# Moving the late weights' low parts from GpSimd to VectorE, and re-queuing the transfers around them

## The chip, the core and the metric

The kernel runs on one core of one Trainium2 chip. The metric is the device time of one launch in microseconds (us). The engines are TensorE (PE in the profile; PEld is its weight load), VectorE (DVE), ScalarE (ACT), GpSimd (POOL) and SyncE (SP), which issues DMAs only. ScalarE and GpSimd can issue DMAs too.

## The reference

Three stages follow one another on 2304 tokens of 512 columns, all in float32:

```
x = decay_attention(q, k, v, f)                  # 4 batches, 8 heads, 576 positions, 64 columns
h = x @ w_in                                     # 512 -> 2048
y = mish(h) @ moe_w_out                          # 2048 -> 512;  mish(h) = h * tanh(softplus(h))
z = max(y @ w1, y @ w2, y @ w3) @ moe2_w_out     # 512 -> 768 -> 512
```

The weights arrive as 8-byte floats.

## The kernel before

**Products.** TensorE multiplies pairs of float32r tiles. Every operand is split into a high part (a rounded copy) and a low part (the value less the high part), and `mm3` (L183 to L187) adds three products per block: high by high, high by low, low by high.

**Weights.** `load_f32` (L148) fetches a chunk of raw words, two int32 each (tile `wr`, three buffers), and five VectorE operations (L161, L162, L165, L168, L172) make float32 of it (tile `wt`, two buffers). `split` (L136) then makes the high part on ScalarE (L138) and the low part on GpSimd (L144).

**Stages.** Attention and the product with `w_in` run interleaved until about 412 us. The rest of `h` follows; each block is copied out as `he` by ScalarE (L544) and stored to `h_d` in DRAM. Meanwhile 16 chunks of `moe_w_out` (128x512) are loaded and split through `in_turn` (L584): a chunk is converted, and the split of the chunk before it is issued behind the last `he` copy (`issue_after`).

The y stage then makes 72 steps (the loop after L670). A step loads a tile `g` of `h_d` (L656, L658, SyncE's queue, six buffers), applies Mish in place (L659, ScalarE), makes `gh` (L665, ScalarE) and `gl` (L666, VectorE), and multiplies them with a chunk of `wo` in 12 matmuls. Loads run five steps ahead and splits two. From step 9 on, every second step converts one chunk of the second block's weights (24 of 128x384 into `wa`, 6 of 128x512 into `wo2`). The converted `wa` chunks are also stored to `a_d` by ScalarE's queue. When a block of 512 tokens is done, four tiles `ze` (three buffers) are copied out of PSUM: for the first block by ScalarE (L697), for the others by ScalarE and VectorE in turn (L703, L700), with the stores to `z_d` on those tiles' own queues, ScalarE's and SyncE's.

The last stage multiplies the first 512 tokens directly (tiles g of L185 to L187 with `yh`, `yl`), and the rest by a scheme of seven products that needs sums of weight blocks. `sums_of_weights` (L752) reads `a_d` back (tile `r`, L759, SyncE's queue), adds on VectorE (L760), splits each sum in two halves on ScalarE and GpSimd (tile `sk`, two buffers), and stores it to `s_d` (L767, SyncE's queue). There are three matrices, with four loads and four stores each. The products of the scheme read `s` from `s_d` (L847, SyncE's queue); they are the matmuls q<-t,s and q<-b,s. `operands` (L717) prepares the tokens' side.

**Order.** Instructions of an engine, and DMAs of a queue, start in one fixed order. A planner draws it up: it runs through the program with a cost for each operation and takes the ready work of the highest priority. Work under `tc.high_priority(AHEAD)` goes first, and `tc.issue_after(ins)` places the work in its block behind `ins` on the same engine without a wait for its end. At run time the order stands, and whatever waits at the head of a queue holds up everything behind it.

Of the kernel before, what the change touches and what calls it, by code (L numbers as in the profile page):

```python
# [67 lines left out]
def tile_decay_attention__mish_ff__max3_ff(  # L68
# [16 lines left out]
    nc = tc.nc  # L85
# [60 lines left out]
    pace, on_act = [], []  # L146

    def load_f32(pool, srcs, bufs=None, abs_eng="dve", raw="wr"):  # L148

        m, n = len(srcs), srcs[0].shape[1]  # L150
        t = pool.tile([128, m, n], F32, name="wt", tag="wt", bufs=bufs)
        r = pool.tile([128, m, n, 2], I32, name=raw, tag=raw, bufs=3 if pool is not wst else bufs)

        with tc.issue_after(pace[-1].ins) if pace else ExitStack():
            for i, src in enumerate(srcs):
                nc.sync.dma_start(r[:, i].rearrange("p n w -> p (n w)"), src.bitcast(I32))
        lo, hi, ti = r[:, :, :, 0], r[:, :, :, 1], t.bitcast(I32)
        if abs_eng == "act":
            nc.scalar.activation(t, hi.bitcast(F32), AF.Abs)
        else:  # L160
            nc.vector.tensor_scalar(ti, hi, 0x7FFFFFFF, None, op0=ALU.bitwise_and)  # L161
        nc.vector.tensor_scalar(  # L162
            t, t, F32_MIN_AS_HIGH_HALF, F32_MAX_AS_HIGH_HALF, op0=ALU.max, op1=ALU.min
        )
        nc.vector.tensor_scalar(  # L165
            ti, ti, 3, 0x3FFFFFF8, op0=ALU.logical_shift_left, op1=ALU.bitwise_and
        )
        nc.vector.scalar_tensor_tensor(  # L168
            out=ti, in0=hi, scalar=-0x40000000, in1=ti,
            op0=ALU.bitwise_and, op1=ALU.bitwise_or,  # L170
        )
        nc.vector.scalar_tensor_tensor(  # L172
            out=ti, in0=lo, scalar=29, in1=ti,
            op0=ALU.logical_shift_right, op1=ALU.bitwise_or,
        )
        return t

    def load_split(pool, dst_hi, dst_lo, srcs, eng_hi, eng_lo, bufs=None, abs_eng="dve", raw="wr"):
        t = load_f32(pool, srcs, bufs, abs_eng, raw)
        split(dst_hi, dst_lo, t, eng_hi, eng_lo)  # L180
        return t
# [16 lines left out]
    def load_w_in():  # L198
        for fp in range(NFP):
            fs = slice(fp * 256, fp * 256 + 256)  # L200
            for c in range(0, KD, 2):
                blocks = [moe_w_in[d * 128:(d + 1) * 128, fs] for d in (c, c + 1)]
                load_split(
                    wst, wi[fp][:, 0, c:c + 2], wi[fp][:, 1, c:c + 2], blocks, "act", "pool", abs_eng="act"
                )
                yield
            loaded.add(fp)
# [303 lines left out]
    def h_steps():  # L511
# [9 lines left out]
        for n, (i, fp) in enumerate(order):  # L521
# [18 lines left out]
            if n % 2 and done < NT:  # L540
                nc.vector.tensor_copy(he, h)
                queue = nc.sync
            else:
                on_act[:] = [nc.scalar.activation(he, h, AF.Copy)]  # L544
                queue = nc.scalar
# [38 lines left out]
    def in_turn(jobs):  # L584

        last = None
        for src, hi, lo, keep in jobs:
            t = load_f32(stg2, [src])
            if last:
                finish_split(*last)  # L590
            last = (t, hi, lo, keep)
            yield
        finish_split(*last)

    def finish_split(t, hi, lo, keep):
        with tc.issue_after(on_act[-1].ins) if on_act else ExitStack():
            split(hi, lo, t, "act", "pool")
            if keep is not None:
                nc.scalar.dma_start(keep, t[:, 0])

    def load_w_out():
        return in_turn(
# [3 lines left out]
        )  # L606
# [27 lines left out]
    def load_w2():  # L634
# [14 lines left out]
        return in_turn(jobs)  # L649

    def load_g(ib, fp, a):
# [3 lines left out]
        if n == BLK2:  # L655
            nc.sync.dma_start(g, h_d[ib][fp][:, a, :])  # L656
        else:
            nc.sync.dma_start(g.rearrange("p (a n) -> p a n", a=2), h_d[ib][fp][:])  # L658
# [3 lines left out]
    def split_g(g, n, tiles):  # L662
# [3 lines left out]
        latest[:] = [nc.vector.tensor_tensor(out=gl, in0=g, in1=gh, op=ALU.subtract)]  # L666
        return [(t, (gh[:, i * n:(i + 1) * n], gl[:, i * n:(i + 1) * n])) for i, t in enumerate(tiles)]

    latest = []
# [5 lines left out]
    for step, (ib, fp, a) in enumerate(todo):  # L675
# [14 lines left out]
        if step >= 8 and step % 2:  # L690
            with tc.issue_after(latest[-1].ins):
                next(wgen3, None)
        if final:
            for j in range(KD):
                ze = zst.tile([128, n], F32, name="ze", tag="ze")
                if ib == 0:
                    nc.scalar.activation(ze, y[j], AF.Copy)  # L697
                    split(y0[0][:, j], y0[1][:, j], ze, "act", "pool")
                elif j % 2:
                    nc.vector.tensor_copy(ze, y[j])  # L700
                    nc.sync.dma_start(z_d[ib][:, j, :], ze)
                else:
                    nc.scalar.activation(ze, y[j], AF.Copy)  # L703
                    nc.scalar.dma_start(z_d[ib][:, j, :], ze)
    for _ in wgen3:
        pass

# [44 lines left out]
    def sums_of_weights(pool):  # L752

        for m in range(3):
            r = {}
            for i in range(2):
                for j in range(2):
                    r[i, j] = pool.tile([128, 2, 384], F32, name=f"r{i}{j}")
                    nc.sync.dma_start(r[i, j], a_d[m][i, j][:])  # L759
            two = lambda o, x, y, op: nc.vector.tensor_tensor(out=o, in0=x, in1=y, op=op)  # L760

            def keep(k, src):
                t = pool.tile([128, 3, 2, 2, 128], F32R, name="sk", bufs=2)
                for c in range(2):
                    with tc.issue_after(on_act[-1].ins):
                        split(t[:, :, c, 0], t[:, :, c, 1], src[:, c].rearrange("p (a f) -> p a f", a=3), "act", "pool")
                nc.sync.dma_start(s_d[m][k][:], t.bitcast(F32))  # L767
# [39 lines left out]
    for ft in range(NF2):  # L807
# [7 lines left out]
        with tc.high_priority(AHEAD):  # L815
# [5 lines left out]
            nc.vector.tensor_tensor(out=hl[ft], in0=mx, in1=hh[ft], op=ALU.subtract)  # L821
# [113 lines left out]
```

## Time and profile before

| | us |
|---|---|
| median of 3 runs (991.92 to 993.0) | 992.31 |
| profiled execution, its own time | 999.44 |
| its span | 997.7 |

| engine | busy us | share of the span |
|---|---|---|
| PE | 927.6 | 93% |
| PEld | 829.1 | 83% |
| DVE | 612.3 | 61% |
| ACT | 472.2 | 47% |
| POOL | 380.7 | 38% |

The mean granted TensorE clock was 0.974 of full speed. The profiled execution has 1.7 us around its span and is 7.1 us longer than the median of the runs without a profile. Shares are means over stages with different limits.

### The profile page before, as it was taken

What the parts mean: (1) busy time and instruction counts of PE and PEld (TensorE: products, weight loads), DVE (VectorE), ACT (ScalarE), POOL (GpSimd) and SP (SyncE); (2) the same over time, 40 slices, a digit from 0 to 9 for tenths busy, and PEclk for the clock granted to TensorE, in tenths of its full rate; (3) what the DMA queues carried; (4) which work ended last, traced back from release to release, by engine and by line L of the source; (5) the groups of instructions that cost most, each with busy time, mean ns of one, the idle gap of its engine ahead of it and who ended that gap; (6) DMA issues with size and microseconds to landing.
All of it is one profiled execution on the core that took longest, in us unless ns stands there. A gap on an engine that the chain in (4) does not pass through costs nothing.

```text
span 997.7 us, 16274 instructions
## 1 busy us (share of the span) xinstructions
PE 927.6 (93%) x5648; PEld 829.1 (83%) x5648; DVE 612.3 (61%) x1299; ACT 472.2 (47%) x1043; POOL 380.7 (38%) x427
## 2 busy tenths in 40 slices
PE   4886789999998999999999989899998999999998
PEld 4674689999998999999878777677886899889986
DVE  4868897755556647339947757577585244814440
ACT  4876666766667666433345444335343222512211
POOL 6766876656446733223304211122135332103310
PEclk8998789999999999999989999999999999999999
DMA  5455646445444531566644656665359744424411
GB/s 154 138 154 149 174 136 195 147 141 156 127 121 138 151 94 43 203 228 201 216 137 158 205 187 185 207 205 169 101 189 334 260 122 119 121 91 121 118 41 74
DMA packets 120130, 154.84 MB, mean 155 GB/s; under 512 B 35888, under 2 KB 79408, under 8 KB 120048
## 3 DMA queue, kind: packets, MB, share of 16 engines
q1 hardware_dynamic: 101360, 130.47, 42.9%
q10 hardware_dynamic: 18688, 23.34, 6.6%
q8 instruction: 44, 0.72, 0.3%
q14 instruction: 38, 0.31, 0.1%
HBM read 107.55 MB, written 46.21 MB: 154 GB/s over the span
## 4 chain that ended last, share of the span: by engine, by line
PE 52%; DVE 17%; DMA 16%; ACT 6%; issue 5%; POOL 2%; SPq 2%; ACTq 0%; DVEq 0%; POOLq 0%
DMA g<-h_d 9%; PE q L185 5%; PE q L186 5%; PE q L187 5%; PE av L453 5%; PE h L186 4%; PE h L185 4%; PE h L187 4%; PE sc L365 3%; PE pp L440 3%; DVE wt L165 3%; DVE wt L168 2%; PE tr L320 2%; PE o L185 2%; PE o L186 2%
## 5 line engine op out<-in xcount | busy, mean ns | idle before, releaser
L185 PE MATMUL h<-xh,wi 128*128 128x256 f32 x576 | 167.1, 291 | 4.3 <-ACT he L544 2.9
L186 PE MATMUL h<-xl,wi 128*128 128x256 f32 x576 | 166.9, 290 | 1.7 <-POOL xl L144 1.7
L187 PE MATMUL h<-xh,wi 128*128 128x256 f32 x576 | 165.8, 288 | 0.0
L186 PE MATMUL y<-gl,wo 128*128 128x512 f32 (+1 forms) x320 | 119.8, 374 | 3.0 <-DVE gl L666 3.0
L187 PE MATMUL y<-gh,wo 128*128 128x512 f32 (+1 forms) x320 | 118.1, 372 | 0.0
L185 PE MATMUL y<-gh,wo 128*128 128x512 f32 (+1 forms) x320 | 107.6, 376 | 9.4 <-ACT gh L665 8.0
L185 PEld LDWEIGHTS h<-xh,wi 128*128 128x128 f32 x576 | 111.3, 194 | 6.0 <-ACT he L544 3.5
L186 PEld LDWEIGHTS h<-xl,wi 128*128 128x128 f32 x576 | 111.4, 193 | 2.8 <-POOL xl L144 2.1
L187 PEld LDWEIGHTS h<-xh,wi 128*128 128x128 f32 x576 | 111.5, 194 | 0.3
L659 ACT ACTIVATE g<-g 128x512 f32<-128x512 f32 x72 | 45.2, 629 | 107.8 <-DMA g<-h_d 102.2
L666 DVE TENSOR_TENSOR gl<-g,gh 128x512 fp32r<-128x512 f32 x72 | 52.8, 734 | 62.0 <-ACT gh L665 61.3
L416 ACT ACTIVATE P<-P,mn 128x128 f32<-128x128 f32 (+3 forms) x128 | 71.0, 556 | 27.2 <-DVE mn L410 26.3
L185 PEld LDWEIGHTS y<-gh,wo 128*128 128x128 f32 x320 | 60.2, 190 | 24.3 <-ACT gh L665 12.7
L144 POOL TENSOR_TENSOR wa<-wt,wa 128x384 fp32r<-128x384 f32 x24 | 26.5, 1103 | 135.3 <-ACT wa L138 135.3
L440 PE MATMUL pp<-ident,P 128*128 128x128 f32 x320 | 61.8, 294 | 14.0 <-POOL P L390 12.8
L186 PEld LDWEIGHTS y<-gl,wo 128*128 128x128 f32 x320 | 61.1, 191 | 15.6 <-DVE gl L666 5.5
L390 POOL TENSOR_SCALAR P<-P,rr 128x128 f32<-128x128 f32 (+3 forms) x128 | 69.1, 555 | 7.0 <-DVE rr L388 3.6
L187 PEld LDWEIGHTS y<-gh,wo 128*128 128x128 f32 x320 | 61.0, 191 | 10.2
L453 PE MATMUL av<-TB,vs 128*128 128x320 f32 (+2 forms) x320 | 61.7, 311 | 4.7 <-ACT TB L447 4.2
L861 DVE TENSOR_TENSOR u<-q,p 128x448 f32<-128x448 f32 x36 | 22.4, 621 | 66.5 <-PE q L187 66.5
L320 PE MATMUL tr<-identr,qk 128*128 128x128 f32 x432 | 49.3, 257 | 13.8 <-POOL qk L144 13.8
L448 DVE TENSOR_TENSOR TB<-pp,TB 128x512 fp32r<-128x512 f32 (+1 forms) x80 | 49.0, 657 | 16.4 <-ACT TB L447 16.0
(147 smaller groups left out, 2357.7 us busy)
## 6 DMA issues: line engine op xcount, KB each, us to landing
g<-h_d SPq DMA_DIRECT2D x72, 256.0 KB, 3.5
s<-s_d SPq DMA_DIRECT2D x72, 256.0 KB, 2.9
h_d<-he ACTq DMA_DIRECT2D x46, 256.0 KB, 3.3
wr<-in_moe_w_out_dram SPq DMA_DIRECT2D x22, 512.0 KB, 4.3
wr<-in_moe_w_dram SPq DMA_DIRECT2D x24, 384.0 KB, 3.4
s_d<-sk SPq DMA_DIRECT2D x12, 768.0 KB, 4.8
cb<-cum_d SPq DMA_DIRECT2D x64, 128.0 KB, 3.4
wr<-in_moe_w_in_dram SPq DMA_DIRECT2D x32, 256.0 KB, 3.6
```

Source lines behind the costliest of these rows:

```text
L165: nc.vector.tensor_scalar(ti, ti, 3, 0x3FFFFFF8, op0=ALU.logical_shift_left, op1=ALU.bitwise_and)
L185: nc.tensor.matmul(ps, wh, xh, start=start, stop=False, skip_group_check=True)
L186: nc.tensor.matmul(ps, wh, xl, start=False, stop=False, skip_group_check=True)
L187: return nc.tensor.matmul(ps, wl, xh, start=False, stop=stop, skip_group_check=True)
L320: nc.tensor.transpose(dst[:, c:c + 128].bitcast(F32R), src, identr)
L390: nc.gpsimd.tensor_scalar(made[ci], made[ci], rr[:, ci:ci + 1], 1.0, op0=ALU.mult, op1=ALU.mult)
L416: nc.scalar.activation(Pt, Pt, AF.Exp, scale=-1.0, bias=mn[:, col - 1:col], accum_out=sm[:, ci:ci + 1],)
L440: nc.tensor.transpose(pp[:, n * 128:n * 128 + 128], Pt[:, k0:k0 + 128], ident)
L448: nc.vector.tensor_tensor(out=T[:, 1, cols], in0=src, in1=T[:, 0, cols], op=ALU.subtract)
L453: nc.tensor.matmul(avp[h][:, off:off + w], vl, T[:, i, c:c + w], start=kt == 0 and i == 0 and not (g == 0 and h == 1), stop=last and i == ...
L659: nc.scalar.activation(g, g, AF.Mish)
L666: latest[:] = [nc.vector.tensor_tensor(out=gl, in0=g, in1=gh, op=ALU.subtract)]
```

## The change

- `load_f32` becomes two functions: `fetch` issues the raw loads, `convert` does the five operations.
- For `moe_w_out` and the second block's weights the low part is made by VectorE, behind the conversion of the next chunk.
- Raw words are fetched two chunks ahead for `moe_w_out` and one ahead for the second block, there behind the last issued load of `g` (`pace`).
- The conversion and the low part are queued behind the last `gl` (or `hl`) on VectorE (`on_dve`), the high part behind the last `gh` (or `hh`) on ScalarE (`on_act`). While `moe_w_out` is loaded both lists are empty.
- All `ze` copies, and for the later blocks the `z_d` stores, go to ScalarE and its queue.
- The sums' loads and stores go to POOL's queue, which issued no DMA before. A sum is split in one operation each by ScalarE and VectorE.

```diff
-    def load_f32(pool, srcs, bufs=None, abs_eng="dve", raw="wr"):
+    pace, on_act, on_dve = [], [], []
+    def fetch(pool, srcs, bufs=None):
...
+        with queued(pace):
             for i, src in enumerate(srcs):
                 nc.sync.dma_start(r[:, i].rearrange("p n w -> p (n w)"), src.bitcast(I32))
+        return r
+    def convert(pool, r, bufs=None, abs_eng="dve"):
...
+    def queued(last):
+        return tc.issue_after(last[-1].ins) if last else ExitStack()
...
-                on_act[:] = [nc.scalar.activation(he, h, AF.Copy)]
+                nc.scalar.activation(he, h, AF.Copy)
...
-    def in_turn(jobs):
+    def in_turn(jobs, ahead, abs_eng):
+        raws, last = [], None
+        def finish_split(t, hi, lo, keep):
+            with queued(on_act):
+                nc.scalar.activation(hi, t, AF.Copy)
+                if keep is not None:
+                    nc.scalar.dma_start(keep, t[:, 0])
+            nc.vector.tensor_tensor(out=lo, in0=t, in1=hi, op=ALU.subtract)
+        for k, job in enumerate(jobs):
+            for src, *_ in jobs[len(raws):k + ahead + 1]:
+                raws.append(fetch(stg2, [src]))
+            with queued(on_dve):
+                t = convert(stg2, raws[k], abs_eng=abs_eng)
+                if last:
+                    finish_split(*last)
+            last = (t, *job[1:])
             yield
...
     def load_w_out():
...
+        return in_turn(jobs, 2, "dve")
     def load_w2():
...
-        return in_turn(jobs)
+        return in_turn(jobs, 1, "dve")
...
-            nc.sync.dma_start(g, h_d[ib][fp][:, a, :])
+            pace[:] = [nc.sync.dma_start(g, h_d[ib][fp][:, a, :])]
...
-            with tc.issue_after(latest[-1].ins):
-                next(wgen3, None)
+            next(wgen3, None)
...
                 ze = zst.tile([128, n], F32, name="ze", tag="ze")
+                nc.scalar.activation(ze, y[j], AF.Copy)
                 if ib == 0:
-                    nc.scalar.activation(ze, y[j], AF.Copy)
                     split(y0[0][:, j], y0[1][:, j], ze, "act", "pool")
-                elif j % 2:
-                    nc.vector.tensor_copy(ze, y[j])
-                    nc.sync.dma_start(z_d[ib][:, j, :], ze)
                 else:
-                    nc.scalar.activation(ze, y[j], AF.Copy)
                     nc.scalar.dma_start(z_d[ib][:, j, :], ze)
...
-                    nc.sync.dma_start(r[i, j], a_d[m][i, j][:])
+                    nc.gpsimd.dma_start(r[i, j], a_d[m][i, j][:])
...
-                for c in range(2):
-                    with tc.issue_after(on_act[-1].ins):
-                        split(t[:, :, c, 0], t[:, :, c, 1], src[:, c].rearrange("p (a f) -> p a f", a=3), "act", "pool")
-                nc.sync.dma_start(s_d[m][k][:], t.bitcast(F32))
+                src = src.rearrange("p c (a f) -> p a c f", a=3)
+                with queued(on_act):
+                    nc.scalar.activation(t[:, :, :, 0], src, AF.Copy)
+                with queued(on_dve):
+                    nc.vector.tensor_tensor(out=t[:, :, :, 1], in0=src, in1=t[:, :, :, 0], op=ALU.subtract)
+                nc.gpsimd.dma_start(s_d[m][k][:], t.bitcast(F32))
```

## Rows read from the trace of the kernel before

**Rows 1.** The page, part 1: busy time, share, instructions.

```profile
PE 927.6 (93%) x5648; PEld 829.1 (83%) x5648; DVE 612.3 (61%) x1299; ACT 472.2 (47%) x1043; POOL 380.7 (38%) x427
```

**Rows 2.** What TensorE waited for, 400 to 998 us: total, times, longest.

```profile
PE y L185 <- ACT gh L665: 8.0, 9, 2.5
PE q L185 <- DMA s<-s_d: 4.2, 1, 4.2
PE y L186 <- DVE gl L666: 3.0, 4, 2.0
```

**Rows 3.** Busy time by stretch: engines, clock, DMA share, GB/s.

```profile
430.00:440.00 10.00, 7.95 (x54) 7.75 (x53) 1.90 (x4) 3.46 (x6) 1.07 (x2) 0.83 0.72 266
500.00:507.00 7.00, 6.42 (x16) 5.08 (x17) 3.15 (x4) 3.41 (x6) 1.28 (x1) 0.54 0.45 144
507.00:520.00 13.00, 13.00 (x59) 10.70 (x58) 4.58 (x10) 6.06 (x10) 0.00 (x0) 1.00 0.33 112
540.00:700.00 160.00, 150.32 (x682) 120.66 (x681) 111.06 (x183) 70.30 (x131) 31.08 (x27) 1.00 0.60 188
770.00:780.00 10.00, 10.00 (x40) 8.30 (x40) 4.62 (x4) 4.12 (x9) 5.90 (x6) 0.87 1.01 404
```

**Rows 4.** Timeline of VectorE while w_out is converted.

```profile
447.06 0.43 DVE L161 TENSOR_SCALAR wt<-wr 128x512 int32<-128x512 int32 x1 [15.09 <-POOL wo L144]
...
462.09 0.42 DVE L161 TENSOR_SCALAR wt<-wr 128x512 int32<-128x512 int32 x1
...
463.01 1.48 DVE L165 TENSOR_SCALAR wt<-wt 128x512 int32<-128x512 int32 x1
...
465.86 0.42 DVE L161 TENSOR_SCALAR wt<-wr 128x512 int32<-128x512 int32 x1
```

**Rows 5.** Timeline of GpSimd (POOL), same stretch.

```profile
438.84 1.05 POOL L140 TENSOR_SCALAR xh<-xr 128x1024 fp32r<-128x1024 f32 x1 [17.90 <-PE h L187]
...
462.92 1.29 POOL L144 TENSOR_TENSOR wo<-wt,wo 128x512 fp32r<-128x512 f32 x1 [2.48 <-ACT wo L138]
```

**Rows 6.** Timeline of TensorE at the last conversions.

```profile
497.86 0.73 PE L185 MATMUL y<-gh,wo 128*128 128x512 f32 x2 [0.78 <-ACT gh L665]
500.58 0.80 PE L186 MATMUL y<-gl,wo 128*128 128x512 f32 x1 [1.98 <-DVE gl L666]
```

**Rows 7.** Chain that ended last, 500 to 720 us: start, us, what.

```profile
559.46 0.70 DVE gl L666
560.18 3.26 DMA g<-h_d
...
577.03 0.70 DVE gl L666
...
585.30 3.90 DMA z_d<-ze
589.33 0.69 DVE ze L700
```

**Rows 8.** Tile g, 540 to 620 us: landing times of its loads.

```profile
DMA to landing us min/median/max: 2.6/3.6/5.3
```

**Rows 9.** VectorE's groups by shape, 540 to 700 us.

```profile
L161 DVE TENSOR_SCALAR wt<-wr 128x384 int32<-128x384 int32 x20 | 21.9, 1094 | 1.1 <-DMA a_d<-wt 1.1
...
L172 DVE SCALAR_TENSOR_TENSOR wt<-wr,wt 128x384 int32<-128x384 int32 x20 | 11.2, 558 | 0.7
L165 DVE TENSOR_SCALAR wt<-wt 128x384 int32<-128x384 int32 x20 | 7.2, 360 | 0.6
...
L700 DVE COPY ze<-y 128x512 f32<-128x512 f32 x6 | 4.1, 686 | 3.2 <-DMA z_d<-ze 3.2
```

**Rows 10.** What SyncE's queue waited for, 700 to 800 us.

```profile
SPq L767 <- POOL sk L144: 26.5, 9, 8.0
```

**Rows 11.** Timeline of SyncE's queue, 750 to 790 us.

```profile
763.57 3.69 SPq L847 DMA_DIRECT2D s<-s_d  x5
```

**Rows 12.** The page, part 6: DMA issues, KB, us to landing.

```profile
wr<-in_moe_w_out_dram SPq DMA_DIRECT2D x22, 512.0 KB, 4.3
```

More of the change, by code (lines that the diff above doesn't have):

```diff
@@ L144, in split @@
         return eng.tensor_tensor(out=dst_lo, in0=src, in1=dst_hi, op=ALU.subtract)
-    pace, on_act = [], []
-    def load_f32(pool, srcs, bufs=None, abs_eng="dve", raw="wr"):
+    pace, on_act, on_dve = [], [], []
+    def fetch(pool, srcs, bufs=None):
         m, n = len(srcs), srcs[0].shape[1]
-        t = pool.tile([128, m, n], F32, name="wt", tag="wt", bufs=bufs)
-        r = pool.tile([128, m, n, 2], I32, name=raw, tag=raw, bufs=3 if pool is not wst else bufs)
-        with tc.issue_after(pace[-1].ins) if pace else ExitStack():
+        r = pool.tile([128, m, n, 2], I32, name="wr", tag="wr", bufs=3 if pool is not wst else bufs)
+        with queued(pace):
             for i, src in enumerate(srcs):
                 nc.sync.dma_start(r[:, i].rearrange("p n w -> p (n w)"), src.bitcast(I32))
+        return r
+    def convert(pool, r, bufs=None, abs_eng="dve"):
+        t = pool.tile([128, r.shape[1], r.shape[2]], F32, name="wt", tag="wt", bufs=bufs)
         lo, hi, ti = r[:, :, :, 0], r[:, :, :, 1], t.bitcast(I32)
@@ L176, in load_f32 @@
         return t
[L178 to L181, printed above, removed]
+    def queued(last):
+        return tc.issue_after(last[-1].ins) if last else ExitStack()
     def mm3(ps, whl, xhl, start, stop):
@@ L202, in load_w_in @@
                 blocks = [moe_w_in[d * 128:(d + 1) * 128, fs] for d in (c, c + 1)]
-                load_split(
-                    wst, wi[fp][:, 0, c:c + 2], wi[fp][:, 1, c:c + 2], blocks, "act", "pool", abs_eng="act"
-                )
+                t = convert(wst, fetch(wst, blocks), abs_eng="act")
+                split(wi[fp][:, 0, c:c + 2], wi[fp][:, 1, c:c + 2], t, "act", "pool")
                 yield
@@ L582, in tile_decay_attention__mish_ff__max3_ff @@
     yps = sb.enter_context(tc.tile_pool(name="yps", bufs=5, space=PSUM, side="right", reuse_waits="tile"))
-    def in_turn(jobs):
[L586 to L591, printed above, removed]
-            yield
[L593 to L599, printed above, removed]
+    def in_turn(jobs, ahead, abs_eng):
[14 more added lines that the diff above has]
+            last = (t, *job[1:])
+            yield
+        with queued(on_dve):
+            finish_split(*last)
     def load_w_out():
-        return in_turn(
+        jobs = [
             (moe_w_out[fp * 256 + a * 128:fp * 256 + a * 128 + 128, :],
@@ L605, in load_w_out @@
             for fp in range(NFP) for a in range(2)
-        )
+        ]
+        return in_turn(jobs, 2, "dve")
     wgen2 = load_w_out()
@@ L665, in split_g @@
         on_act[:] = [nc.scalar.activation(gh, g, AF.Copy)]
-        latest[:] = [nc.vector.tensor_tensor(out=gl, in0=g, in1=gh, op=ALU.subtract)]
+        on_dve[:] = [nc.vector.tensor_tensor(out=gl, in0=g, in1=gh, op=ALU.subtract)]
         return [(t, (gh[:, i * n:(i + 1) * n], gl[:, i * n:(i + 1) * n])) for i, t in enumerate(tiles)]
-    latest = []
     wgen3 = load_w2()
@@ L706, in tile_decay_attention__mish_ff__max3_ff @@
         pass
+    pace.clear()
     HALF = (NT - BLK2) // 4
@@ L763, in keep @@
                 t = pool.tile([128, 3, 2, 2, 128], F32R, name="sk", bufs=2)
-                for c in range(2):
-                    with tc.issue_after(on_act[-1].ins):
-                        split(t[:, :, c, 0], t[:, :, c, 1], src[:, c].rearrange("p (a f) -> p a f", a=3), "act", "pool")
-                nc.sync.dma_start(s_d[m][k][:], t.bitcast(F32))
+                src = src.rearrange("p c (a f) -> p a c f", a=3)
+                with queued(on_act):
+                    nc.scalar.activation(t[:, :, :, 0], src, AF.Copy)
+                with queued(on_dve):
+                    nc.vector.tensor_tensor(out=t[:, :, :, 1], in0=src, in1=t[:, :, :, 0], op=ALU.subtract)
+                nc.gpsimd.dma_start(s_d[m][k][:], t.bitcast(F32))
             two(r[1, 1], r[1, 0], r[1, 1], ALU.add)
@@ L820, in tile_decay_attention__mish_ff__max3_ff @@
             on_act[:] = [nc.scalar.activation(hh[ft], mx, AF.Copy)]
-            nc.vector.tensor_tensor(out=hl[ft], in0=mx, in1=hh[ft], op=ALU.subtract)
+            on_dve[:] = [nc.vector.tensor_tensor(out=hl[ft], in0=mx, in1=hh[ft], op=ALU.subtract)]
         next(sgen, None)
```

2 lines of the change are left out of this document (1 added, 1 removed).

## The prediction, made before the changed kernel ran

> **What bounds the kernel now.** I start with the page's busy times: TensorE works 93% of the span [rows 1], so time can be won only where it stands idle or runs at a lower clock. Next, the list of its waits from 400 us on, where the change acts. They are few: `gh` from ScalarE 8.0 us, `gl` from VectorE 3.0, and one wait of 4.2 for the weight sums `s` [rows 2]. A table by stretch then says where they lie and adds the clock [rows 3]. Three losses lie within reach of the change.
>
> First, the end of the `w_out` conversions. TensorE waits 0.78 us for `gh` and 1.98 for `gl` [rows 6], and after that runs at a granted clock of 0.54 from 500 to 507 us, most of it at the lower of its two levels, 1.2 GHz; that is 7 x 0.46 = 3.2 us of work not done [rows 3]. Together 6.0 us. The timelines show why `gl` is late: VectorE converts chunk after chunk until 500 us, in periods of 465.86 - 462.09 = 3.77 us [rows 4]. Two things make that late. It stood still for 15.09 us before 447.06, waiting for GpSimd to give back a `wt` buffer [rows 4], and GpSimd's queue stood behind `xh`, which waited 17.90 us for TensorE [rows 5]. And in each period one VectorE operation takes 1.48 us instead of 0.42 to 0.43, while GpSimd runs a low part of 1.29 us [rows 4, 5].
>
> Second, the y stage. From 540 to 700 us TensorE is busy 150.3 of 160 us at full clock: 9.7 lost [rows 3]. The chain of the latest work shows a ring there: `gl` frees a buffer of `g`, the load goes out at once, lands, Mish and `gh` run, then the next `gl`. Three turns from 559.46 to 577.03 are 5.86 us each [rows 7], and a turn advances two steps. TensorE needs 24 matmuls for these, at 13.0 / 59 = 0.22 us about 5.3 us [rows 3]. So the ring is slightly too slow. At block ends it also passes through a `z_d` store (3.90) and a `ze` copy (0.69) [rows 7].
>
> Third, the sums: 4.2 us of waiting [rows 2] and a clock of 0.87 for 10 us after it, 1.3 us: 5.5. The loads of `s` stood in SyncE's queue until 763.57 [rows 11], behind stores of sums that waited 26.5 us in total for GpSimd [rows 10].
>
> **Part 1, `w_out`.** Removed from the path: GpSimd's 16 low parts, and with them the 15.09 us wait and the stretched operation, 1.48 - 0.42 = 1.06 us per chunk. Added to VectorE: a low part. No row shows one of 128x512 from two float32 tiles on this line, but `gl` is the same operation and shape, 0.70 [rows 7]. New period: 3.77 - 1.06 + 0.70 = 3.41. The chunk that began at 447.06 can begin up to 15.09 earlier, at 432, and the 14 from there end at 432 + 14 x 3.41 = 479.7 instead of 500. If ScalarE's queue delays the high parts and nothing of the 15.09 is won, they end at 447.1 + 47.7 = 494.8. Either is before TensorE asks at 497.9, so `gh` and `gl` no longer queue behind conversions. I take the whole 6.0; the low end, 3, is one late `gl` with its low clock. The raw loads are no limit: three buffers of 3.41 us give 10.2 us for a landing of 4.3 [rows 12]. What VectorE newly waits for is ScalarE's high part, and behind that wait stand the next conversion and `gl`; the high part has a whole conversion of 2.7 us to be done, so this costs nothing unless ScalarE itself stands still. The stretch from 430 to 440 us (2.05 us idle, clock 0.83 [rows 3]) stays: the `he` copies are where they were.
>
> **Part 2, the ring of the y stage.** VectorE loses the stretched operations, 20 x (1094 - 360) ns = 14.7 us, and the `ze` copies, 4.1 us; it gains 20 low parts near the 558 ns of the two-tensor operation of their shape [rows 9] and 5 near 0.70, together 14.7. So VectorE ends 4 us lighter on 111 [rows 3]: no new bound. The raw load moves from just before a pair of `g` loads to just behind the first of a pair. The landing of `g` ranges from 2.6 to 5.3 us, median 3.6 [rows 8]; the ring turns in 5.86 with about the median, so 2.6 would give 4.9, under TensorE's 5.3, and the whole 9.7 would come back; if the second `g` of the pair now stands behind the raw words it may come to 4.7 instead, and nothing does. The `ze` wait for a store (3.90) moves from VectorE to ScalarE, where Mish and `gh` stand behind it; both are links of the ring, so I count it as even (bounds: four block ends by 3.9, 16 us either way). SyncE's queue loses its `z_d` stores, and `g` loads no longer stand behind them. Between 0 and 9.7 I take 4.
>
> **Part 3, the sums.** SyncE's queue loses 12 loads and 12 stores; POOL's queue gets them. The loads of `s` then wait for their own stores only. VectorE gains 12 low parts of 128x768, at 0.70 x 768 / 512 about 1.05 us each (an estimate from the `gl` row), GpSimd loses 24. Both bounds: 5.5 back, or nothing, if the transfers themselves were the limit: the DMA share is 1.01 right behind the wait [rows 3]. I take 5, as SyncE's own waits of 26.5 us name the queue. What one issue on POOL's queue costs no row shows: between nothing and the 1.29 us of a low part [rows 5], 24 x 1.29 = 31 us spread over some 60 us in which GpSimd has little else.
>
> The Trainium skill, "DMA: Bandwidth & Descriptors", section "Issuing engines are not separate DMA queues", says that DMAs of all issuing engines run on the same 16 DMA engines and interleave, so that another issuer saves only issue time. By that, part 3 frees the queue's head, and brings nothing if the wait was for bandwidth; the share of 1.01 speaks for it, the 26.5 us against.
>
> **The sum.** 6.0 + 4 + 5 = 15.0 us, set against the profiled execution's 999.4: 984.4. The runs' median stands at 992.31 / 999.44 = 0.9929 of it: 977.4 us.
>
> **Rivals.**
>
> *Only part 1 pays* (the ring and the transfers stay as slow). For it: the ring's load takes most of its turn, and the DMA share of 1.01. Against it: the waits in SyncE's queue. 999.4 - 6.0 = 993.4, as a run 986.4.
>
> *The low part becomes a link of the ring* (slower). If the planner's order puts ScalarE's high part behind a Mish that waits for its load, VectorE's low part stands still with it and the next `gl` comes a low part later: 30 chunks by about 0.6 us = 18 us, less 11.0 from the other parts: 1006.4, as a run 999.3. It decides from 11.0 / 30 = 0.37 us per chunk on. Against it: a low part only fills what the stretch gave up.
>
> *POOL's queue is late* (slower). The first `s` needs four loads and four stores through that queue. With 1.29 us each, and each behind one VectorE operation of 1.48, that is 8 x 2.77 = 22 us, added to the wait for `s`: 999.4 - 10.0 + 22 = 1011, as a run 1004. It decides from 10 us on, 1.25 per transfer. Against it: few operations of the sort that was stretched run in that stage. Beside it stands a rule of the Trainium skill, "SBUF — State Buffer", section "SBUF: two separate sides": GpSimd itself writes the descriptors of DMAs from its queue, and cannot while VectorE runs an operation on both ports, so such a DMA waits. It advises the queues that part 3 leaves. No row of the kernel before shows a DMA on that queue.
>
> *Nothing moves.* TensorE's wait for `gl` comes from another link, or the order shifts a stall elsewhere: 992.
>
> **Chances.** The forecast 0.52 (its own range 971 to 983), only part 1 0.22, low part in the ring 0.12, POOL's queue 0.06, nothing 0.08. About 0.2% (2 us) is what a measurement of this kernel can tell from no change. Faster: 0.52 + 0.22 = 0.74; the same: 0.08 and a little of the two slow rivals where they only cancel the gain, 0.10; slower 0.16. The range takes forecast, part 1 and nothing. Below, all three in full are 6.0 + 9.7 + 5.5 = 21.2, which is 978.2 or 971.3 as a run; with the loss of 2.05 and 1.7 at 430 to 440 as well 967.6. So 967 to 994.
>
> **What would show it.** Right: no VectorE wait for GpSimd near 447, conversion periods near 3.4, no `gl` wait of TensorE near 500 and a clock of 1.00 there; L161 at 0.36 throughout; y-stage idle time of TensorE near 6 us; `s` loads out by 757 and no wait for them. Wrong: turns of the ring at or over 5.9, ScalarE standing before the fourth `ze`, VectorE before low parts, or `s` waiting for stores that left POOL's queue late.

## The result, and the profile after

The changed kernel takes 966.68 us (median of 4 runs, 963.98 to 967.01) against 992.19 for the kernel before (4 runs): ratio 0.9736, 95% interval 0.9717 to 0.9754. That is 25.5 us faster; the prediction said 14.9 faster (977.4, range 967 to 994). The direction held, the size did not.

The profiled execution of after took 963.98 us (span 962.2), 35.5 less than that of before (999.44). Some 10 us of this are the two executions' own: the one of before lies 7.2 above its median, the one of after 2.7 below. A second profile of each kernel stands below, as before_again and after_again, and shows which of the readings repeat.

What TensorE waits for from 400 to 970 us; columns as in [rows 2], whose three waits are gone (the one row left out is 0.5 us):

```profile
PE h L187 <- POOL xl L144: 1.2, 1, 1.2
PE g L186 <- ACT mx L821: 0.9, 1, 0.9
PE q L187 <- DVE t L144: 0.7, 1, 0.7
```

Busy time by stretch, columns as in [rows 3] (after's work lies up to 35 us earlier from 520 us on):

```profile
430.00:440.00 10.00, 10.00 (x71) 9.35 (x70) 7.62 (x15) 5.24 (x11) 3.61 (x2) 1.00 0.81 280
500.00:507.00 7.00, 7.00 (x33) 5.79 (x32) 3.83 (x8) 2.46 (x5) 0.00 (x0) 1.00 0.45 145
507.00:520.00 13.00, 13.00 (x59) 10.78 (x58) 8.87 (x20) 7.07 (x13) 0.00 (x0) 1.00 0.65 208
540.00:700.00 160.00, 159.08 (x790) 135.05 (x789) 105.10 (x211) 78.55 (x146) 2.37 (x4) 1.00 0.60 197
770.00:780.00 10.00, 10.00 (x51) 9.15 (x50) 5.72 (x10) 2.92 (x6) 6.08 (x5) 1.00 0.51 146
```

The stretch at 430 us, which the prediction let stand at 7.95 us and 0.83, is full. So is 500 to 507. From 540 to 700 us TensorE shows 159.08 of 160 us busy, and 790 matmuls; before it showed 150.32 and 682 [rows 3].

These two counts can't be set against each other, as the end of after's window holds shorter matmuls. The whole stretch from the end of `h` to the end of `y` can: first before, then after (of the engines, here and below, TensorE alone).

```profile
488.60:712.40 223.80, 211.37 (x987) 0.98 0.54 172
```

```profile
487.20:683.30 196.10, 196.06 (x954) 1.00 0.58 191
```

Before needed 27.7 us more, for 33 matmuls more. A step of after takes 2.72 us for 12 matmuls (the chain below), 0.2267 each, so the 33 are worth 7.5 us; 20.2 us were lost against after. The same stretch in the second profiles, before_again and after_again:

```profile
486.20:707.40 221.20, 209.95 (x987) 0.99 0.56 174
```

```profile
493.60:693.35 199.75, 197.22 (x954) 1.00 0.59 188
```

Here the loss is 21.45 - 7.5 = 14.0 us. The two pairs differ by 6 us, so the first is no more exact than that. In the first about 6.0 are the end of `w_out`, as the prediction summed it, and 14.2 the y stage. In the second the end of `w_out` is some 4.3 (2.59 us idle from 490 to 500 us, clocks of 0.92 and 0.91 from 490 to 510), and 9.7 are the y stage. The prediction had bounded the y stage by the idle time from 540 to 700 us, 9.7. A busy column does not show the whole of such a loss. From 540 to 660 us, first before, then after:

```profile
540.00:660.00 120.00, 112.90 (x484) 1.00 0.61 190
```

```profile
540.00:660.00 120.00, 120.00 (x533) 1.00 0.65 214
```

Before shows 7.1 us idle, but 49 matmuls are missing, and at 120 / 533 = 0.225 us these are 11.0. In the second pair the busy times differ by 5.0 us and the counts by 33 matmuls, 7.4 us. The row of one matmul is 0.39 us long and the next starts 0.23 after it, so a short gap hides inside the busy time.

VectorE's timeline at the `w_out` conversions, which answers to [rows 4], and its groups by shape from 540 to 700 us, which answer to [rows 9]:

```profile
438.83 1.41 DVE L175 SCALAR_TENSOR_TENSOR wt<-wr,wt 128x512 int32<-128x512 int32 x1
440.17 2.90 DVE L593 TENSOR_TENSOR wo<-wt,wo 128x512 fp32r<-128x512 f32 x1
...
478.90 0.69 DVE L593 TENSOR_TENSOR wo<-wt,wo 128x512 fp32r<-128x512 f32 x1 [0.70 <-ACT wo L590]
```

```profile
L593 DVE TENSOR_TENSOR wa<-wt,wa 128x384 fp32r<-128x384 f32 x18 | 9.9, 552 | 0.0
...
L164 DVE TENSOR_SCALAR wt<-wr 128x384 int32<-128x384 int32 x17 | 6.0, 354 | 0.0
```

The last low part starts at 478.90 us (the prediction worked out an end at 479.7; after_again has it at 484.94). Two operations are still stretched, at 438.83 and 440.17, while GpSimd splits a block of x. In the y stage the first conversion step takes 0.354 us instead of 1.094, and the low part 0.552.

The chain that ended last, 515 to 660 us, by line, and three of its pieces; in [rows 7] it ran through `gl` and the loads of `g`:

```profile
by line: PE y L188 31.7%; PE y L186 31.7%; PE y L187 31.6%; PE g L188 1.8%; PE g L186 1.8%; PE g L187 1.7%
...
541.41 0.45 PE y L186 x2
544.13 0.45 PE y L186 x2
546.85 0.45 PE y L186 x2
```

It is TensorE throughout, and a step begins every 2.72 us: in this execution the ring no longer sets the pace. In after_again it still does in part: 53.7% of the chain over the same window are loads of `g`, and TensorE does 626 matmuls there, where after does 643 and before 594.

The sums: SyncE's queue, which answers to [rows 11] (start, time to the last of the group, count), and tile `sk` on POOL's queue.

```profile
718.78 79.39 SPq L851 DMA_DIRECT2D s<-s_d  x32
```

```profile
L771 POOL DMA_DIRECT2D s_d<-sk x12: 531/542/551, 701.4 to 747.5; - x12
...
DMA to landing us min/median/max: 3.9/5.1/7.9
```

Loads of `s` leave from 718.78 us on. In before one left at 759.60, and the next stood until 763.57.

One part of the 35.5 us was no effect of the change. These are the last waits of attention in TensorE's timeline of before, of after, and of the same changed kernel in another execution (it stands below as after_again):

```profile
411.90 0.39 PE L186 MATMUL h<-xl,wi 128*128 128x256 f32 x1 [0.94 <-POOL xl L144]
```

```profile
407.66 0.39 PE L187 MATMUL h<-xl,wi 128*128 128x256 f32 x1 [1.17 <-POOL xl L144]
```

```profile
414.02 0.38 PE L187 MATMUL h<-xl,wi 128*128 128x256 f32 x1 [1.18 <-POOL xl L144]
```

Attention ended 4.2 us earlier in after's profile and 2.1 later in the other, so this is scatter between executions (before_again has its last wait at 411.51).

### The profile page after: what moved, and what is told of

Same layout as the page of the kernel before. It is cut to its first block, busy times and chain, and to the rows that moved or that the text cites. A ratio compares the mean times of both kernels' runs of the same rounds, so it can differ in the third digit from the quotient of the medians.

```text
span 962.2 us, 16234 instructions
## 1 busy us (share of the span) xinstructions
PE 915.0 (95%) x5648; PEld 823.8 (86%) x5648; DVE 592.9 (62%) x1349; ACT 474.6 (49%) x1039; POOL 312.6 (32%) x381
## 4 chain that ended last, share of the span: by engine, by line
PE 77%; DVE 8%; DMA 5%; ACT 3%; issue 2%; POOL 2%; SPq 1%; ACTq 0%; DVEq 0%; POOLq 0%
PE y L186 7%; PE y L188 7%; PE y L187 7%; PE h L187 6%; PE h L186 6%; PE h L188 6%; PE q L187 5%; PE q L188 5%; PE q L186 5%; PE av L453 4%; PE sc L365 3%; PE pp L440 3%; PE o L186 2%; PE o L187 2%; PE o L188 2%; PE tr L320 2%
## 5 line engine op out<-in xcount | busy, mean ns | idle before, releaser
L186 PEld LDWEIGHTS h<-xh,wi 128*128 128x128 f32 x576 | 109.9, 191 | 3.3 <-DVE he L541 1.7
L188 PEld LDWEIGHTS h<-xh,wi 128*128 128x128 f32 x576 | 110.0, 191 | 0.3
L673 DVE TENSOR_TENSOR gl<-g,gh 128x512 fp32r<-128x512 f32 x72 | 50.3, 698 | 79.4 <-ACT gh L672 79.3
L761 POOL DMA_DIRECT2D r<-a_d x12 | 6.7, 558 | 159.9 <-ACT b L138 159.3
```

The source lines that it names most:

```text
L186: nc.tensor.matmul(ps, wh, xh, start=start, stop=False, skip_group_check=True)
L188: return nc.tensor.matmul(ps, wl, xh, start=False, stop=stop, skip_group_check=True)
L673: on_dve[:] = [nc.vector.tensor_tensor(out=gl, in0=g, in1=gh, op=ALU.subtract)]
```

## The experiments

Theories. **G**: GpSimd's low parts made the losses, at `w_out` and in the y stage, through stretched VectorE operations and late buffers. **L**: the order of the raw loads did. **S**: SyncE's queue did, with the sums and the stores of `y` in it. The experiments are the changed kernel with a part put back, or the kernel before with a part alone. Each ratio is to the kernel before on the same chip; rows of a batch share a chip.

| batch, kernel | median us | ratio | 95% interval |
|---|---|---|---|
| 1 before_again | 995.34 | 0.9987 | 0.9966 to 1.0009 |
| 1 lo_on_pool | 982.54 | 0.9857 | 0.9824 to 0.9889 |
| 1 fetch_undone | 970.24 | 0.9742 | 0.9709 to 0.9774 |
| 1 sums_undone | 973.10 | 0.9764 | 0.9740 to 0.9788 |
| 2 after_again | 970.96 | 0.9753 | 0.9692 to 0.9814 |
| 2 lo_alone | 976.45 | 0.9829 | 0.9793 to 0.9866 |
| 2 w2_lo_on_pool | 977.36 | 0.9836 | 0.9798 to 0.9874 |
| 2 ze_undone | 970.50 | 0.9764 | 0.9703 to 0.9826 |
| 3 lo_he | 978.25 | 0.9816 | 0.9794 to 0.9838 |
| 3 behind_he | 972.67 | 0.9755 | 0.9737 to 0.9772 |
| 3 fetch_ze_undone | 969.64 | 0.9738 | 0.9700 to 0.9776 |
| 3 wi_lo_dve | 969.88 | 0.9737 | 0.9697 to 0.9777 |
| 4 wout_lo_on_pool | 977.27 | 0.9812 | 0.9780 to 0.9845 |
| 4 sums_ze_undone | 977.88 | 0.9831 | 0.9793 to 0.9869 |
| 4 sums_queue_undone | 974.01 | 0.9780 | 0.9746 to 0.9814 |
| 4 sums_lo_undone | 976.83 | 0.9798 | 0.9756 to 0.9840 |

In these batches times scatter more than in the first measurement (before: 989.62 to 999.53 in 33 runs), so a difference between two rows counts only beside both intervals, which reach 2 to 6 us either way. The first measurement of after has 0.9717 to 0.9754.

One stretch of the profiles is read beside the medians below, "the last stretch": from the last matmul of `y` to the end. It takes 278.9 us in after and in after_again, 285.3 in before and 287.5 in before_again.

### What one chip repeats

**before_again** is the kernel before, unchanged.

> The kernel before, unchanged, for a second profile of it. Its profiled execution of 999.4 us was 7 us longer than the runs. If that profile is typical, a second one shows the same losses: about 20 us of TensorE's idle time and low clock between 412 and 770 us. If part of it belonged to that one execution, the second profile comes out near 992 us, and the places that lack the loss are to be named.

It gave 0.9987, and its profile shows the same waits as [rows 2]: `gh` 8.0 us, `s` 4.6, `gl` 1.9. The stall near 433 us is smaller in it: 1.6 us idle from 430 to 440 us, at a clock of 1.00. **after_again** is the changed kernel.

> The changed kernel as it is, on one chip with the next three, so that each is set against it. Every theory expects its first ratio, 0.972 to 0.975 of the kernel before, and in its profile no wait of y for gh or gl between 440 and 660 us.

0.9753: the gain repeats. The expected "no wait" did not quite hold: `y` waits 1.0 us for `gh` once, and 1.5 for `ze`.

### The late weights' low parts (theory G)

**lo_on_pool**: the low parts of `w_out` and w2 on GpSimd again, all else as changed.

```diff
-            nc.vector.tensor_tensor(out=lo, in0=t, in1=hi, op=ALU.subtract)
+            nc.gpsimd.tensor_tensor(out=lo, in0=t, in1=hi, op=ALU.subtract)
```

> The changed kernel, with the low parts of moe_w_out and of the second block's weights made by GpSimd again; everything else as changed. GpSimd theory (the y stage was freed because VectorE's operations are no longer stretched by GpSimd's and its buffers no longer wait for GpSimd): both the late conversions (6 us) and most of the y stage's idle time (10 us) come back, 978 to 985 us. Load theory (the y stage was freed because the raw loads stand behind the loads of g): only the late conversions come back, 970 to 974 us, and the y stage stays without waits of TensorE.

0.9857: nearly half of the gain is gone, some 12 us. **lo_alone** is the other side, the kernel before with that edit only.

```diff
-            split(hi, lo, t, "act", "pool")
+            split(hi, lo, t, "act", "dve")
```

> The kernel before with one edit: the low parts of w_out and w2 are made by VectorE. Put back alone in the changed kernel they had cost some 12 us of 25 (0.9857 against 0.9736). If the parts of the change add up, this edit alone brings the same 12 us, 0.986 to 0.990 of before, and the other 13 lie in other edits. If the low parts on GpSimd are the cause of nearly everything and the rest of the change only keeps them from mattering, it brings 18 us or more, 0.982 or less. If VectorE then holds up the ring of the y stage, as one of the rivals in the prediction has it, it brings less than 6 us, 0.994 or more, and TensorE's waits for gl in the y stage grow.

0.9829, some 17 us of the 25 from one word. What TensorE still waits for, and its stretches:

```profile
PE q L185 <- DMA s<-s_d: 4.2, 1, 4.2
PE h L185 <- ACT he L544: 2.4, 1, 2.4
```

```profile
430.00:440.00 10.00, 7.63 (x51) 0.83 0.72 265
570.00:630.00 60.00, 60.00 (x265) 1.00 0.70 219
750.00:780.00 30.00, 30.00 (x140) 0.98 0.68 243
```

The y stage is full (60.00 of 60 us). Two losses stand, the stall at 433 us and the wait for `s` with its lower clock after. So the parts do not add up: put back in the changed kernel the low parts cost 12 us, alone they bring 17.

**w2_lo_on_pool** and **wout_lo_on_pool** put back one of the two groups of weights each (`in_turn` takes the engine of the low part as an argument).

```diff
-            nc.vector.tensor_tensor(out=lo, in0=t, in1=hi, op=ALU.subtract)
+            low.tensor_tensor(out=lo, in0=t, in1=hi, op=ALU.subtract)
...
-        return in_turn(jobs, 1, "dve")
+        return in_turn(jobs, 1, "dve", nc.gpsimd)
```

> The changed kernel with the low parts of w2 alone on GpSimd again, those of w_out stay on VectorE. The prediction split its gain as 6 us for w_out and 4 for the y stage. If the cost of GpSimd's low parts lies in the y stage (VectorE's stretched operations in the ring), this gives back 6 to 10 of the 12 us: ratio to before 0.980 to 0.984, and the waits of y for gh and gl come back from 540 us on. If it lies at the end of the w_out conversions, it gives back 0 to 4 us: 0.974 to 0.978, and TensorE stays fully busy from 540 to 660 us.

> The changed kernel with the low parts of w_out alone on GpSimd again, those of w2 stay on VectorE. Both together lost some 12 us (0.9857), those of w2 alone 8 (0.9836 beside 0.9753 on one chip). If the two add up, this loses 3 to 5 us, 0.977 to 0.980, all of it between 425 and 510 us, and TensorE is fully busy from 520 to 650 us. If a delay at the end of w_out is taken up by the y stage, which has time to spare without GpSimd, it loses nothing, 0.972 to 0.976; if w2 alone had made the whole loss by chance of the order, the same.

Measured 0.9836 (8 us beside after_again) and 0.9812 (6 to 8 us beside the two measurements of after, more than expected). For w2 the first expectation held; waits of 2.8 us for `gh` and 1.2 for `gl` are back. VectorE, GpSimd and ScalarE of w2_lo_on_pool in one turn of the ring, then VectorE of after in one:

```profile
604.60 0.69 DVE L673 TENSOR_TENSOR gl<-g,gh 128x512 fp32r<-128x512 f32 x1 [2.38 <-ACT gh L672]
605.21 1.17 DVE L164 TENSOR_SCALAR wt<-wr 128x384 int32<-128x384 int32 x1
...
607.80 0.56 DVE L175 SCALAR_TENSOR_TENSOR wt<-wr,wt 128x384 int32<-128x384 int32 x1
608.28 0.68 DVE L673 TENSOR_TENSOR gl<-g,gh 128x512 fp32r<-128x512 f32 x1
```

```profile
605.06 1.11 POOL L593 TENSOR_TENSOR wa<-wt,wa 128x384 fp32r<-128x384 f32 x1 [5.75 <-ACT wa L590]
```

```profile
605.63 0.62 ACT L672 ACTIVATE gh<-g 128x512 fp32r<-128x512 f32 x1
```

```profile
597.51 0.35 DVE L164 TENSOR_SCALAR wt<-wr 128x384 int32<-128x384 int32 x1
597.78 0.55 DVE L593 TENSOR_TENSOR wa<-wt,wa 128x384 fp32r<-128x384 f32 x1
...
599.50 0.68 DVE L673 TENSOR_TENSOR gl<-g,gh 128x512 fp32r<-128x512 f32 x1
600.11 0.55 DVE L175 SCALAR_TENSOR_TENSOR wt<-wr,wt 128x384 int32<-128x384 int32 x1
```

GpSimd's low part starts at 605.06, and VectorE's step issued behind it takes 1.17 us, 0.82 more than the 0.35 in after. `gh` is ready at 606.25, but `gl` starts at 608.28, behind the whole conversion. In after `gl` runs between two steps of the conversion. Over 525 to 665 us a `gl` came up to 2.2 us behind its `gh` with GpSimd, up to 1.2 without. How much of that is the stretch and how much the changed place of `gl` in the order was not separated.

For `w_out` the place held for the most part: 57 of 60 us busy from 450 to 510 us, 60 from 510 to 570. The mechanism was not among those expected. VectorE, ScalarE, and TensorE's wait:

```profile
446.20 1.50 DVE L164 TENSOR_SCALAR wt<-wr 128x512 int32<-128x512 int32 x1 [1.16 <-POOL wo L593]
...
462.20 1.48 DVE L168 TENSOR_SCALAR wt<-wt 128x512 int32<-128x512 int32 x1
```

```profile
451.13 0.64 ACT L590 ACTIVATE wo<-wt 128x512 fp32r<-128x512 f32 x1 [3.17 <-DVE wt L175]
451.67 0.58 ACT L544 ACTIVATE he<-h 128x512 f32<-128x512 f32 x1
```

```profile
PE h L186 <- ACT he L544: 4.4, 5, 1.6
```

VectorE waits for a `wt` buffer that GpSimd still reads and then runs stretched. ScalarE's high part waits 3.17 us for that conversion, the `he` copy stands behind it, and TensorE waits for `he`, 4.4 us in five waits.

### The order of the raw loads (theory L) and the copies of y

**fetch_undone** loads raw words beside their conversion again, without `pace`.

```diff
-        return in_turn(jobs, 2, "dve")
+        return in_turn(jobs, 0, "dve")
...
-            pace[:] = [nc.sync.dma_start(g, h_d[ib][fp][:, a, :])]
+            nc.sync.dma_start(g, h_d[ib][fp][:, a, :])
```

> The changed kernel, with each raw load issued beside its own conversion and not queued behind the loads of g, as before; the low parts stay on VectorE. Load theory: landings of g back at a median of 3.6 us or more in the y stage, TensorE's waits for gh back, 975 to 982 us. GpSimd theory: within 2 us of the changed kernel's 966.7.

0.9742: nothing lost, and `y` waits 1.5 us for `gh`, beside 1.0 in after_again. L is refuted. **ze_undone** returns every second `ze` copy to VectorE and its store to SyncE's queue.

```diff
-                nc.scalar.activation(ze, y[j], AF.Copy)
...
+                elif j % 2:
+                    nc.vector.tensor_copy(ze, y[j])
+                    nc.sync.dma_start(z_d[ib][:, j, :], ze)
```

> The changed kernel with every second copy of y on VectorE and its store on SyncE's queue again. The prediction counted this edit as even, with bounds of 16 us either way. If the stores in SyncE's queue or the copies on VectorE held up the loads of g, this loses 3 to 8 us: ratio to before 0.977 to 0.982, with waits of y for gh right behind the block ends. If the edit is even, 0.972 to 0.976.

0.9764 beside 0.9753: even, as far as these runs tell. **fetch_ze_undone** undoes both, so that neither can cover for the other.

> The changed kernel without two of its parts at once: each raw load beside its conversion again, and every second copy of y on VectorE with its store on SyncE's queue. Each alone lost at most some 2 us. If the two are even because neither bears on the ring once GpSimd is out, this gives 0.973 to 0.978 of before. If each only covers for the other (one keeps the loads of g early enough alone), both together lose 6 us or more, 0.980 or higher, with waits of y for gh from 510 to 660 us.

0.9738. Both parts are worth nothing that these medians can show, as long as the others stand.

The profiles lean against the new `ze` inside the y stage. From 515 to 660 us TensorE does 634 to 639 matmuls in the five kernels with the old copies and the low parts on VectorE (lo_alone, lo_he, ze_undone, fetch_ze_undone and sums_ze_undone). It does 609 to 627 in seven that have all copies on ScalarE (after_again, fetch_undone, behind_he, wi_lo_dve and three of the sums), and waits there 0.8 to 2.9 us for `gh`. The profile of after, with 643, is the exception. Between the means lie 16 matmuls, some 4 us; with one execution of each this is a sign, not a measurement.

### The stall at 433 us

The prediction said that this loss stays. **lo_he** is lo_alone with the `he` copy no longer noted in `on_act`; **behind_he** is the changed kernel with it noted again.

```diff
-                nc.scalar.activation(he, h, AF.Copy)
+                on_act[:] = [nc.scalar.activation(he, h, AF.Copy)]
```

> The kernel before with two edits: low parts of w_out and w2 on VectorE, and the copies he no longer hold back the high parts of w_out. With the low parts alone (0.9829 of before), two losses were left in the stages of the change: 2.4 us of waiting for he near 433 us with a granted clock of 0.83 from 430 to 440, and 4.2 us of waiting for s. If the order behind he makes the first, it goes here, 2.4 and 1.7 us: ratio 0.977 to 0.980, and TensorE is fully busy from 430 to 440 us; the wait for s stays. If the stall at 433 us comes from the loads of g alone, as the prediction took it (it said that this loss stays), the ratio stays at 0.982 to 0.985.

> The changed kernel with one line put back: the copies he again hold back the high parts of w_out. The same question from the other side. If that line makes the stall near 433 us, it returns: TensorE waits 2 us or more for he between 425 and 440 us, and the ratio to before is 0.977 to 0.980. If not, 0.972 to 0.976.

TensorE's stretches in lo_he:

```profile
420.00:450.00 30.00, 30.00 (x224) 1.00 0.84 292
450.00:510.00 60.00, 57.54 (x391) 0.97 0.57 180
```

The stall at 433 us went (30.00 of 30), and another came between 450 and 510 us: 2.5 us idle and a clock of 0.97. The ratio, 0.9816, did not move from 0.9829. In behind_he (0.9755) TensorE waits 0.9 us for `he`, not the 2 expected, and 2.9 for `gh` later. So the line decides where ScalarE's order stalls TensorE, and no gain of its own was seen.

### The sums (theory S)

**sums_undone** has loads and stores in SyncE's queue and GpSimd's low parts in halves again; **sums_queue_undone** the queues alone, **sums_lo_undone** the low parts alone; **sums_ze_undone** is sums_undone and ze_undone together.

```diff
-                    nc.gpsimd.dma_start(r[i, j], a_d[m][i, j][:])
+                    nc.sync.dma_start(r[i, j], a_d[m][i, j][:])
...
-                with queued(on_act):
-                    nc.scalar.activation(t[:, :, :, 0], src, AF.Copy)
-                with queued(on_dve):
-                    nc.vector.tensor_tensor(out=t[:, :, :, 1], in0=src, in1=t[:, :, :, 0], op=ALU.subtract)
-                nc.gpsimd.dma_start(s_d[m][k][:], t.bitcast(F32))
+                for c in range(2):
+                    with queued(on_act):
+                        split(t[:, :, c, 0], t[:, :, c, 1], src[:, c].rearrange("p (a f) -> p a f", a=3), "act", "pool")
+                nc.sync.dma_start(s_d[m][k][:], t.bitcast(F32))
```

> The changed kernel, with the weight sums as before: loads and stores on SyncE's queue, low parts in halves on GpSimd. The prediction's part 3 says the wait for s (4.2 us) and the low clock after it come back: 971 to 973 us. The rival, that the transfers' bandwidth was the limit and the wait went because everything before it ended earlier, says no change: 965 to 969 us.

> The changed kernel with loads and stores of the sums in SyncE's queue again; the low parts of the sums stay on VectorE. If SyncE's queue was what held the loads of s (the prediction's reading of its 26.5 us of waiting), part of the loss of the sums edit is here: loads of s leave 3 us or more later than in the changed kernel, 0.975 to 0.978. If GpSimd's low parts were what the queue waited for, moving them is enough: 0.972 to 0.975.

> The other half: the low parts of the sums on GpSimd again, 24 of some 1.25 us, with the loads and stores of the sums on GpSimd's queue between them. If GpSimd's queue is then late, as one rival in the prediction has it, s comes later and TensorE waits for it: 0.980 or more. If the transfers have time to spare there, 0.973 to 0.977.

> The changed kernel without the edit of the sums and without that of ze: sums through SyncE's queue with GpSimd's low parts, every second copy of y on VectorE and its store on SyncE's queue. Undone alone, each lost at most 3 us, and TensorE did not wait for s. If the old sums are late only when y's stores stand in SyncE's queue as well, the wait for s is back, 3 to 5 us, with a granted clock below 1.00 in the 20 us after it: 0.979 to 0.983. If the two are separate, they lose 2 to 5 us together, 0.975 to 0.979, and no wait for s comes.

Alone, the old sums cost 1 to 3 us (0.9764), TensorE does not wait for `s`, and the last stretch takes 279.6 us. With the old `ze` as well the wait is back. SyncE's queue and TensorE's wait in sums_ze_undone:

```profile
740.57 0.40 SPq L853 DMA_DIRECT2D s<-s_d  x1
743.69 0.32 SPq L773 DMA_DIRECT2D s_d<-sk  x1
...
744.58 3.90 SPq L853 DMA_DIRECT2D s<-s_d  x5
```

```profile
PE q L186 <- DMA s<-s_d: 4.4, 1, 4.4
```

One load of `s` leaves at 740.57; the next five stand behind the store of 743.69 until 744.58. The chain has a landing of 5.82 us there, to 750.40, and TensorE starts at 750.44. The same queue in sums_undone:

```profile
736.93 1.41 SPq L849 DMA_DIRECT2D s<-s_d  x2
...
739.85 3.14 SPq L849 DMA_DIRECT2D s<-s_d  x4
```

There the loads leave at 736.93 and 739.85, and TensorE's first product with `s`, at 742.60, waits for nothing. The time of sums_ze_undone is 0.9831: 8 us beside after_again, where each part alone lost at most 3. That batch has no changed kernel in it, but the last stretch agrees: 288.3 us, against 279.6 in sums_undone, 280.6 in ze_undone and 278.9 in after. The two parts cover for each other: with `y`'s stores out of SyncE's queue the old sums come early enough, and with the sums on POOL's queue `y`'s stores do no harm. In sums_ze_undone the first loads of `r` wait 4.5 us for a store of `y` to land and leave at 699.76; in sums_undone they leave at 694.75. Whether the store in SyncE's queue or the copy on VectorE makes the delay was not separated. This is the last third of the gain: lo_he, which has both in the old form, stands at 0.9816 with a wait of 4.4 us for `s`; fetch_ze_undone, with the new sums, at 0.9738 on the same chip without one.

The halves, 0.9780 and 0.9798, overlap each other's intervals and that of sums_undone, so the times leave open which half matters. In the last stretch the queues alone cost nothing (278.9 us) and the low parts alone 4.8 (283.7). With the low parts on GpSimd the wait that came was not for `s` but for `hl` and `hh` of the product after it:

```profile
PE o L188 <- DVE hl L823: 1.7, 2, 1.3
PE o L186 <- ACT hh L822: 1.1, 1, 1.1
```

### The same lever once more

**wi_lo_dve** moves the low parts of `moe_w_in`, during attention, to VectorE too.

```diff
-                split(wi[fp][:, 0, c:c + 2], wi[fp][:, 1, c:c + 2], t, "act", "pool")
+                split(wi[fp][:, 0, c:c + 2], wi[fp][:, 1, c:c + 2], t, "act", "dve")
```

> The changed kernel with the same lever applied once more, during attention: the low parts of moe_w_in, 16 operations of 1.36 us on GpSimd, are made by VectorE. In the changed kernel the two-input operations of that conversion take 0.91 and 0.98 us where they take 0.69 in the y stage, so some of them are stretched. If GpSimd beside VectorE costs time wherever it runs, 2 to 6 us are won on the changed kernel, 0.967 to 0.972 of before. If only those stretches count that lie in a ring on which TensorE waits, nothing is won, 0.972 to 0.976; if VectorE, busy 75 to 92 per cent of the first 150 us, becomes the bound there, it loses, 0.977 or more.

0.9737, no change. That fits the view that a stretched operation costs only where a ring that TensorE waits for runs through it, but this run alone does not show it. No version tried beats the changed kernel by more than the intervals.

## Why the prediction was right in direction and wrong in size

**Part 1, 6.0 us: right in size, though not by one path, and the match of the end is partly luck.** The waits for `gh` and `gl` near 500 us and the low clock after them went, and wout_lo_on_pool costs 6 to 8 us. The last 14 conversions, however, begin at 427.49 us in after and not at 432, with a period of 3.65 us and not 3.41, so that 479.7 was met by two errors that cancel. In wout_lo_on_pool most of the loss went through ScalarE's `he` copies, a link that the prediction did not have.

**Part 2, "Between 0 and 9.7 I take 4": the step that failed.** The prediction saw the ring and GpSimd's stretch. But it set the stretch only against VectorE's load ("no new bound") and let the landing of `g` decide what comes back, with the raw load's place in SyncE's queue for or against it. The landing hardly moved: its median from 540 to 620 us is 3.6 us in before, 3.3 in after, 3.3 in lo_alone and 3.4 in fetch_undone. fetch_undone shows that the place is worth nothing; lo_alone shows the y stage full with the old order of loads. What paid was GpSimd's low parts out of VectorE's way, and the term measured 14.2 us in the first pair of profiles and 9.7 in the second, not 4. The bound of 9.7, idle time of a busy column, lies below the loss in the profile that it was read from. With GpSimd out of the ring, a step takes the 12 matmuls of 0.2267 us, 2.72, and in after the ring keeps up; in after_again it does not quite, 3.6 us over the whole stretch.

**"The stretch from 430 to 440 us stays": wrong.** It went in after, 2.05 us idle and 1.7 of clock [rows 3]. lo_he shows that such a stall can also move on, and before_again has a smaller one, so this is not a sure 3.8 us.

**Part 3, 5 us: the wait was the right one, but it was not the sums' alone.** The wait for `s` and its low clock went; the last stretch is 6.4 us shorter in the first pair and 8.6 in the second. But the `ze` stores, which the prediction counted as even, would have been enough for most of it by themselves (sums_undone), and so would the sums edit (ze_undone). The prediction priced each part against the kernel before, where two queued causes of one wait can't be seen apart.

**The sum.** By stretch, in us won; the 7.5 us of the 33 matmuls that after does before the end of `h` are set over.

| stretch | predicted | before to after | before_again to after_again |
|---|---|---|---|
| attention, to its last wait for `xl` | 0 | 4.2 | -2.5 |
| from there to the end of `h` | 0 | 4.6 | 2.6 |
| end of `h` to end of `y` | 10.0 | 20.2 | 14.0 |
| from there to the end | 5 | 6.4 | 8.6 |
| whole span | 15.0 | 35.5 | 22.7 |

Attention's row is scatter. Without it the second pair gives 25.2, close to the 25.5 of the medians; in the first some 6 us more fell to the y stage. So the prediction lacked 4 to 10 us in the y stage, 3 to 5 before it and 1 to 4 at the sums.

**The rivals.** That only part 1 pays is refuted by w2_lo_on_pool. That the low part becomes a link of the ring and makes the kernel slower is refuted by lo_alone. That POOL's queue comes late is refuted in after: stores on it take 0.531 to 0.551 us to issue, and TensorE does not wait for `s`. The Trainium skill, "SBUF — State Buffer", section "SBUF: two separate sides", warns that a DMA from GpSimd's queue stands while VectorE holds the ports that both share; the issue of these 12 stores does not show it. Of a GpSimd operation and a VectorE operation that takes those ports the same section of the Trainium skill says that the one that starts second waits for the other's end, and there the trace agrees: VectorE's step issued at 605.21 ends at 606.38, 0.21 us after GpSimd's low part (605.06 and 1.11).

## What to carry to other kernels

Where an engine keeps pace with a ring of short steps, bound the loss by the count of finished matmuls in a known stretch, not by the idle time of its busy column, and take two profiles of each kernel: here the same stretch gave 20.2 and 14.0 us. A second engine's low-priority operations can cost far more than their own time if they lengthen an operation that a ring runs through; the same operations during attention (wi_lo_dve) cost nothing that was measured. Before pricing the parts of a change one by one, look for two that feed the same queue: undone singly both seem worth little, undone together they cost some 8 us.

## What the runs showed of the hardware that was not expected

In after a load of `s`, 256 KB, issued by SyncE takes 0.32 us of its queue (median); a store of 768 KB issued by GpSimd takes 0.54 us of GpSimd, and it lands in 5.1 us (medians). That is 24 issues of some 0.55 us, 13 us of GpSimd in all, where the prediction allowed up to 31.

The profile's busy column for TensorE hides gaps: 7.1 us shown idle from 540 to 660 us in the kernel before, 11.0 by the count of matmuls against after.
